# A guess of an expert computed outside the third attention, and three sums moved from GpSimd to VectorE, in a fused attention and mixture-of-experts kernel

## The chip, the core and the metric

The kernel runs on 1 core of one Trainium2 chip. The metric is the device time of one execution in microseconds (us). Before the change three runs took 357.07, 357.61 and 358.25 us; the median is 357.61.

## What is computed

The reference is grouped-query attention (8 batches, 16 heads of queries, 4 of keys and values, 384 positions, 64 per head), whose output goes, row by row, through a mixture of 4 × 4 experts with two gates. Cut to its core:

```python
scores = np.matmul(q, k.transpose(0, 1, 3, 2)) / np.sqrt(D)     # k, v repeated for 4 heads each
attn = np.exp(scores - scores.max(-1, keepdims=True))
x = np.matmul(attn / attn.sum(-1, keepdims=True), v)            # -> rows of 1024
g_idx = np.argmax(x @ w_group, axis=1)                          # a group, then an expert of it
e_idx = np.argmax(xg @ w_expert[g], axis=1)
ye = np.maximum(xg @ w1[g, e], 0.0) @ w2[g, e]
out[tok] = g_w * e_w * ye                                       # softmax weights of the two picks
```

## The kernel before

The work is staged by batch. The attention of a batch has 24 **units** (`NU`; 4 key heads times 6 blocks of 64 keys). A unit is a score step (`score`, L318: four 64x64 matmuls into a PSUM tile "s", then one exponential on ScalarE, L324, which writes `e`) and a product with v (`pv`, L337). `Attn.run` puts the score of unit u + 2 ahead of the product of unit u, so TensorE works while ScalarE takes exponentials; there are two "s" tiles, so the score of unit u + 2 can start only when the exponential of unit u has been read. "s" tiles are shared with the hidden layer and the output of the experts, "o" tiles with the outputs of attention. The name "x" gives the "o" tile that is not in use at that moment.

The sums of the softmax are taken from `e`: GpSimd adds the two units of a pair (`pair`, L345), VectorE reduces the pair (`reduce`, L354); units listed in `apart` are not added on GpSimd, and VectorE reduces both units of the pair itself (pair u holds units u - 1 and u). `join_keys` (L407) adds the parts, `sums` (L416) adds over partitions with TensorE and takes reciprocals, `normalise` (L455, L459) multiplies, `cast` (L464, or L466 on GpSimd) makes the bf16 copy `xb` that the experts read, a quarter of the 1024 columns at a time.

The experts' weights (2 MB each for w1 and w2) are loaded for one expert per batch, and that expert is *guessed* before the gate is known: the sum of v over the keys (`vsum`) goes through TensorE (`guess_mean`, L480), VectorE copies the result (`vm`, L482), TensorE multiplies it with the gate matrix (`guess_logits`, L487), VectorE picks the expert (`pick_guess`, L568 to L581) and GpSimd reads its number (`read_pick`) and issues the loads. Any pick of the real gate that the guess did not cover is computed in a loop at the end.

The order on every engine is written out by hand: the dictionaries `steps0`, `steps1` and `steps2` list what follows the product of a unit in the first three attentions (2: after unit 2; 4.5: after unit 4, ahead of its pair and reductions), `lags` says behind which unit a pair is reduced. The expert layers of batch b run behind the attention of batch b + 1, except the first hidden layer (`moe_h(0, ...)`), which stands in the second attention behind unit 17. `first_block` holds what lies between the second and the third attention: the first outputs of batch 0 (`ffn_y`, L650), the sums and the normalisation of batch 1, whose last two quarters GpSimd multiplies. `block(b)` is the same for the later batches. The gate's logits of batch 1 (`second_gate`, L474) stand in the third attention.

`sum_v` (L112 to L114) is the sum of v on GpSimd in three additions; `first_sum_v` (L121) the same on VectorE in one reduction, for batch 0 alone.

Of the kernel before, what the change touches and what calls it, by code (L numbers as in the profile page):

```python
# [18 lines left out]
def kernel(  # L19
# [97 lines left out]

    def first_sum_v():
        vsum[0] = gpool.tile([P, NA * D], BF16, name="vsum")
        with nc.allow_low_precision(reason="the guess of an expert alone reads this"):  # L120
            nc.vector.tensor_reduce(  # L121
                out=vsum[0].rearrange("p (a d) -> p a d", d=D),
                in_=vraw[0].rearrange("p a (c d) -> p a d c", d=D), axis=AX.X, op=ALU.add)

# [286 lines left out]

    def sums(b, g0, g1, which, tiles=False):
        sm = ps_tile(which)[:, :, :(g1 - g0) * 2 * NB]
        for r in range(2):
            if not tiles:
                nc.tensor.matmul(out=sm[:, r], lhsT=half32[:, r, :],  # L416
                                 rhs=red[b][:, g0:g1].rearrange("p g t j -> p (g t j)"),
                                 start=True, stop=True)
                continue
            rs = slice(r * H2, (r + 1) * H2)  # L420
            for t in range(2):
                nc.tensor.matmul(
                    out=sm[t * D:(t + 1) * D, r].rearrange("p (g t j) -> p g t j", t=2, j=NB)[:, :, t],
                    lhsT=half32[rs, r, t * D:(t + 1) * D], rhs=red[b][rs, g0:g1, t],
                    start=True, stop=True)
        if b not in inv:
            inv[b] = gpool.tile([P, KQ, NB], F32, name="inv", bufs=2)
        iv = inv[b][:, 2 * g0:2 * g1].rearrange("p (g r) j -> p r g j", r=2)
        sm = sm.rearrange("p r (g t j) -> p r g t j", t=2, j=NB)
        for t in range(2):  # L430
            ts = slice(t * D, (t + 1) * D)
            nc.vector.reciprocal(out=iv[ts], in_=sm[ts, :, :, t])  # L432

    Q = P // 4
# [35 lines left out]
    def gate_logits(b, pt):  # L470
        for m in range(KQ):
            x = xT[b][:, m, :].rearrange("p (j t x) -> p t j x", t=4, x=32)
            for t in range(4):
                nc.tensor.matmul(out=pt[32 * t:32 * t + 32, 0, :S // 4],  # L474
                                 lhsT=wg[:, head_pair(m), :], rhs=x[:, t],
                                 start=(m == 0), stop=(m == KQ - 1))

    def guess_mean(b, pt):
        pm = pt[:, 1, :2]
        nc.tensor.matmul(out=pm, lhsT=vsum[b], rhs=halfb, start=True, stop=True)  # L480
        vm = gpool.tile([P, 2], BF16, name="vm")
        nc.vector.tensor_copy(out=vm, in_=pm)  # L482
        return vm

# [147 lines left out]
    def ffn_h(x, w1, hT, f0, which):  # L632
        h = ps_tile(which)
        for jj in range(2):
            for m in range(KQ):
                nc.tensor.matmul(out=h[:, jj, :S],  # L636
                                 lhsT=w1[:, head_pair(m), (f0 + jj) * P:(f0 + jj + 1) * P],
                                 rhs=x[:, m, :], start=(m == 0), stop=(m == KQ - 1))
        if f0 + 2 < FQ:
# [41 lines left out]
    def before_attention(b):  # L681

        if b + 1 < B:
# [10 lines left out]
             for i in range(5)]  # L694
# [3 lines left out]
                      22: [17]}),  # L698
        1: Attn(1, apart=(9, 11), act_copies=(2, 3), later=(7, 13, 15, 17), homes=homes,
                lags={18: [13], 19: [15], 20: [17], 22: [19], 23: [21]}),  # L700
# [23 lines left out]
    def x_logits(b):  # L724
# [7 lines left out]
        0: [gate_matrix_2],  # L732
        2: [do(first_q1, "x"), first_sum_v],
        4: [do(first_k, NC, 2 * NC, "x")],
# [23 lines left out]
    def first_fetch():  # L758
# [18 lines left out]
            do(at[1].reduce, 3),  # L777
            do(at[1].reduce, 5),
            x_gate_logits,
            lambda: mean(1, state["pt"]),  # L780
            do(at[1].pair, 7),
            do(at[1].reduce, 7),
            do(moe_h, 0, 2, "s"),
            do(at[1].pair, 13),
            do(at[1].pair, 15),
            first_softmax,
            do(at[1].reduce, 9),
            do(moe_h, 0, 4, "s"),
# [10 lines left out]
    def first_block():  # L799
        load_v(3)  # L800
        moe_y(0, 0, "s")
        sum_v(2)
        load_k(3)
# [3 lines left out]
        y = ffn_y(w2s[0], hTs[0], 1, "s", (0,))  # L807
        sums(1, 0, Hkv, "o")
        ffn_y(w2s[0], hTs[0], 1, "s", (1,), y)
# [5 lines left out]
        ffn_y(w2s[0], hTs[0], 2, "o", (0,), y)  # L815
        at[2] = Attn(2, later=(1,), lags={5: [1], 6: [3], **{u: [u - 2] for u in range(7, NU, 2)}})
        at[2].score(0)
# [3 lines left out]
        normalise(1, 1, None, pool)  # L821
        normalise(1, 3, None, pool)

    def second_gate():
# [5 lines left out]
    steps2 = {  # L830
        1: [do(cast, 1, 2), do(at[2].pair, 1), do(x_mean, 2)],
        2: [do(x_logits, 2)],
        3: [do(cast, 1, 1)],
        4.5: [second_gate],
        6: [do(cast, 1, 3)],
        8: [do(read_pick, 2)],
    }
    at[2].run(steps2)
# [3 lines left out]
    def block(b):  # L842
# [24 lines left out]
        at[b].reduce(NU - 1)  # L867
        join_keys(b, 0, Hkv)
        if b == 2:
# [24 lines left out]
        if ahead:  # L894
            guess_logits(vm, guess_out(pt))
        elif not last:
            vm = guess_mean(b + 1, pt)
        ffn_y(w2s[f], hTs[f], 1, "s", (1,), y)
        y_out(f, 1, y)
        gate_logits(b, pt)  # L900
        if not (last or ahead):
            guess_logits(vm, guess_out(pt))
        if b <= EARLY:
            at[b + 1] = Attn(b + 1)
            at[b + 1].start()
        cast(b, 3)
        w = gate_softmax(b, gate_rows(pt, not last), not last)
# [166 lines left out]
```

## Time and profile before

| | us |
|---|---|
| median of three runs | 357.61 |
| the profiled execution | 356.7 |
| its span, first to last instruction | 354.9 |
| TensorE busy with matmuls | 345.9 (97%) |
| VectorE busy | 253.9 (72%) |
| ScalarE busy | 225.0 (63%) |
| GpSimd busy | 220.2 (62%) |

PE is TensorE's matmuls, PEld its weight loads, DVE VectorE, ACT ScalarE, POOL GpSimd, SP the engine that issues most loads and stores. Matmuls overlap, so the duration of one matmul is longer than the time from its start to the start of the next; what a matmul costs is read from start to start. "Busy" at 97% therefore leaves open whether the matmuls follow each other as fast as they could. A few matmul records are missing from the trace (one expert output block shows 7 or 22 where 8 or 23 were issued).

### The profile page before, as it was taken

The numbers are of one execution on the slowest core, as the hardware profiler recorded it, in microseconds if no ns is written. First come the engines' busy times: TensorE is split into PE (matmuls) and PEld (weight loads), VectorE is DVE, ScalarE is ACT, GpSimd is POOL, SyncE is SP. The second block draws the span as 40 slices with busy tenths as digits, with TensorE's granted clock in tenths as the row PEclk, the third lists the DMA queues.
The fourth block names the chain that finished last, engine by engine and source line by source line (L and its number), as shares of the span: only waits on it lengthen the run. The fifth ranks groups of instructions, "written<-read, shape, count | busy, mean of one in ns | idle before, by whom it ended". The sixth has DMA issues, their size and how long they took to land.

```text
span 354.9 us, 9208 instructions
## 1 busy us (share of the span) xinstructions
PE 345.9 (97%) x3801; PEld 182.5 (51%) x3816; DVE 253.9 (72%) x520; ACT 225.0 (63%) x296; POOL 220.2 (62%) x171
## 2 busy tenths in 40 slices
PE   8999999999999999999999999999999999999994
PEld 4455565445555455554555555545545545555642
DVE  5797769767697777976689667886769677796031
ACT  5899925299536795378954499355982669444311
POOL 7889985869935499308991299804995059900000
PEclk9999999999999999999999999999999999999998
DMA  8979999799989999999999999999995995099925
GB/s 199 215 135 188 220 207 160 134 275 222 193 174 176 258 209 182 206 163 203 229 221 207 193 220 211 218 192 193 228 211 95 197 263 130 2 175 219 258 48 137
DMA packets 69327, 67.15 MB, mean 189 GB/s; under 512 B 37113, under 2 KB 49401, under 8 KB 69281
## 3 DMA queue, kind: packets, MB, share of 16 engines
q0 software_dynamic: 26640, 41.03, 67.2%
q1 hardware_dynamic: 42272, 24.94, 30.4%
q8 instruction: 32, 0.52, 0.6%
q10 hardware_dynamic: 368, 0.54, 0.4%
q14 instruction: 15, 0.11, 0.1%
HBM read 86.07 MB, written 12.58 MB: 278 GB/s over the span
## 4 chain that ended last, share of the span: by engine, by line
PE 87%; ACT 4%; POOL 3%; DVE 2%; issue 1%; DMA 1%; ACTq 0%; SPq 0%; POOLq 0%; DVEq 0%
PE ps_o L337 30%; PE ps_s L636 22%; PE ps_s L650 13%; PE ps_s L318 8%; PE ps_o L650 6%; PE ps_o L474 3%; ACT e L324 2%; POOL w L345 2%; PE ps_o L636 1%; PE ps_s L951 1%; PE ps_o L951 1%; DMA w<-in_q_dram 1%; POOL xb L466 1%; ACT w L324 0%; DVE inv L432 0%
## 5 line engine op out<-in xcount | busy, mean ns | idle before, releaser
L345 POOL TENSOR_TENSOR e<-e 128x768 f32<-128x768 f32 x91 | 162.8, 1826 | 37.0 <-PE ps_s L318 30.8
L324 ACT ACTIVATE e<-ps_s 128x768 f32<-128x768 f32 x187 | 147.7, 813 | 15.0 <-PE ps_s L318 12.8
L337 PE MATMUL ps_o<-e,v_raw 64*64 64x384 f32 x1496 | 150.1, 482 | 0.0
L354 DVE TRANSPOSE_TENSOR_REDUCE red<-e 128x24 f32<-128x768 f32 x95 | 91.4, 972 | 36.7 <-POOL e L345 36.6
L636 PE MATMUL ps_s<-xb,w 128*128 128x384 bf16 x480 | 80.1, 326 | 0.1
L337 PEld LDWEIGHTS ps_o<-e,v_raw 64*64 64x64 f32 x1496 | 55.3, 133 | 35.7 <-issue 29.5
L636 PEld LDWEIGHTS <-w 128*128 128x128 bf16 x512 | 49.4, 98 | 36.4 <-issue 4.5
L318 PE MATMUL ps_s<-qT,kT 64*64 64x384 bf16 x768 | 65.0, 325 | 0.4
L650 PEld LDWEIGHTS <-hT 128*128 128x128 bf16 x336 | 31.5, 98 | 37.7 <-issue 1.5
L650 PE MATMUL ps_s<-w,hT 128*128 128x512 bf16 x217 | 49.5, 379 | 0.4
L640 ACT ACTIVATE hT<-ps_s 128x768 bf16<-128x768 f32 x23 | 18.6, 810 | 46.7 <-PE ps_s L636 43.3
L318 PEld LDWEIGHTS <-kT 64*64 64x64 bf16 x768 | 24.5, 105 | 35.6 <-issue 33.6
L669 ACT ACTIVATE ot<-ps_s,we 128x1024 f32<-128x1024 f32 x14 | 15.6, 1115 | 19.0 <-PE ps_s L650 17.2
L604 POOL COPY tok<-qT 1x1 bf16<-1x1 bf16 x6 | 1.1, 179 | 42.5 <-DMA qT<-q_raw 42.5
L379 DVE COPY xT<-ps_o 128x768 f32<-128x768 f32 x26 | 24.0, 924 | 2.7 <-ACT xb L464 1.5
L455 DVE STREAM_TRANSPOSE e<-inv 128x768 f32<-128x768 f32 x26 | 25.2, 971 | 0.2
L464 ACT CAST xb<-xT 128x768 bf16<-128x768 f32 x28 | 23.1, 830 | 3.4 <-DVE xT L459 3.2
L650 PE MATMUL ps_o<-w,hT 128*128 128x512 bf16 x105 | 24.0, 379 | 1.1 <-issue 1.1
L459 DVE TENSOR_TENSOR xT<-xT,e 128x768 f32<-128x768 f32 x24 | 23.1, 962 | 0.8
L495 DVE STREAM_TRANSPOSE gl<-ps_o 128x96 f32<-128x96 f32 x8 | 2.3, 283 | 18.7 <-PE ps_o L474 15.0
L643 ACT ACTIVATE hT<-ps_s 128x384 bf16<-128x384 f32 x14 | 6.1, 488 | 12.5 <-PE ps_o L480 7.2
L474 PEld LDWEIGHTS ps_o<-xT,wg 128*32 128x32 f32 x448 | 9.2, 110 | 3.3 <-issue 2.1
(140 smaller groups left out, 233.3 us busy)
## 6 DMA issues: line engine op xcount, KB each, us to landing
w<-in_moe_w_dram POOLq DMA_DIRECT2D x16, 2048.0 KB, 21.9
out_dram<-ot SPq DMA_DIRECT2D x42, 256.0 KB, 6.9
q_raw<-in_q_dram POOLq DMA_DIRECT2D x7, 768.0 KB, 11.0
v_raw<-in_v_dram SPq DMA_DIRECT2D x7, 384.0 KB, 5.7
k_raw<-in_k_dram POOLq DMA_DIRECT2D x7, 192.0 KB, 6.4
out_dram<-ot SPq DMA_DIRECT2D x10, 128.0 KB, 2.4
w<-in_q_dram POOLq DMA_DIRECT2D x3, 192.0 KB, 6.3
w<-in_k_dram SPq DMA_DIRECT2D x2, 192.0 KB, 3.7
```

What stands on the lines that cost most here:

```text
L318: nc.tensor.matmul(out=sT[r * H2:(r + 1) * H2, s, :S], lhsT=kT[b][s * D:(s + 1) * D, key_block(b, s, g // 2, c), ks], rhs=qT[b][s * D:(s + ...
L324: nc.scalar.activation(e.rearrange("p t (s x) -> p s t x", s=2), sT[:, :, :S].rearrange("p s (t x) -> p s t x", t=2), ACT.Exp, scale=scale)
L337: nc.tensor.matmul(out=oT[t * D:(t + 1) * D, r, :S], lhsT=vraw[b][r * H2:(r + 1) * H2, g // 2, c * D:(c + 1) * D], rhs=self.e[u][r * H2:(r ...
L345: nc.gpsimd.tensor_add(out=self.e[u - 1], in0=self.e[u - 1], in1=self.e[u])
L354: nc.vector.tensor_reduce(out=red3[b][:, g, parts[b][g]].rearrange("p t j -> p (t j)"), in_=self.e[w].rearrange("p t (j x) -> p (t j) x", ...
L379: nc.vector.tensor_copy(out=dst, in_=src)
L455: nc.vector.transpose(out=rb.rearrange("p k (j x) -> p k j x", x=32), in_=inv[b][:, ks].unsqueeze(3).to_broadcast([P, 2, NB, 32]))
L459: eng.tensor_mul(out=x, in0=x, in1=rb)
L464: nc.scalar.copy(out=xb[b][:, ks, :], in_=xT[b][:, ks, :])
L474: nc.tensor.matmul(out=pt[32 * t:32 * t + 32, 0, :S // 4], lhsT=wg[:, head_pair(m), :], rhs=x[:, t], start=(m == 0), stop=(m == KQ - 1))
L636: nc.tensor.matmul(out=h[:, jj, :S], lhsT=w1[:, head_pair(m), (f0 + jj) * P:(f0 + jj + 1) * P], rhs=x[:, m, :], start=(m == 0), stop=(m == ...
L650: nc.tensor.matmul(out=y[:, nh, :], lhsT=hT[:, f, c * P:(c + 1) * P], rhs=w2[:, f, nh * HALF:(nh + 1) * HALF], start=(f == 0), stop=(f == ...
```

## The change

- **`ffn_h`**: the first hidden block of a batch (`f0` = 0) is summed in two passes: six of eight row blocks of x for both halves of the tile, then the last two for both.
- **The sum of v for batch 2** is taken by VectorE (`reduce_v(2)`) in the second attention, behind unit 17 and ahead of `first_softmax`, in place of GpSimd's `sum_v(2)` in `first_block`. The reductions of units 8 and 9 move ahead of it too.
- **The guess for batch 2**: its product stands in the tile and beside the matmuls of `sums(1, ...)` in `first_block`; in the third attention only the logits are left, behind unit 1 in place of unit 2.
- **Pairs**: 23 of the second attention (units 22 and 23) and 1 of the third (units 0 and 1) are `apart`; the latter was put off by `later` before, and is now reduced behind unit 2.
- **Casts** of batch 1: three quarters, behind units 1, 3 and 6 before, now stand together behind the gate's logits at 4.5.
- **Batch 3's guess** in `block(2)`: product behind the gate's logits, logits behind the first two scores of the next attention.
- Keys of the third attention's first head are joined behind unit 10.

```diff
-    def first_sum_v():
-        vsum[0] = gpool.tile([P, NA * D], BF16, name="vsum")
+    def reduce_v(b):
+        vsum[b] = gpool.tile([P, NA * D], BF16, name="vsum")
...
-    def sums(b, g0, g1, which, tiles=False):
-        sm = ps_tile(which)[:, :, :(g1 - g0) * 2 * NB]
+    def sums(b, g0, g1, which, tiles=False, mean=None):
+        pt = ps_tile(which)
+        sm = pt[:, :, :(g1 - g0) * 2 * NB]
...
+        if mean is not None:
+            guess_product(mean, pt, MEAN)
...
+        return pt if mean is None else guess_copy(pt, MEAN)
...
+    MEAN = 2 * KQ * NB
+
+    def guess_product(b, pt, n):
+        nc.tensor.matmul(out=pt[:, 1, n:n + 2], lhsT=vsum[b], rhs=halfb, start=True, stop=True)
+
+    def guess_copy(pt, n):
+        vm = gpool.tile([P, 2], BF16, name="vm")
+        nc.vector.tensor_copy(out=vm, in_=pt[:, 1, n:n + 2])
+        return vm
...
-        for jj in range(2):
-            for m in range(KQ):
-                nc.tensor.matmul(out=h[:, jj, :S],
...
+        ends = [0, KQ] if f0 else [0, KQ - 2, KQ]
+        for m0, m1 in zip(ends, ends[1:]):
+            for jj in range(2):
+                for m in range(m0, m1):
+                    nc.tensor.matmul(out=h[:, jj, :S],
...
-        1: Attn(1, apart=(9, 11), act_copies=(2, 3), later=(7, 13, 15, 17), homes=homes,
+        1: Attn(1, apart=(9, 11, 23), act_copies=(2, 3), later=(7, 13, 15, 17), homes=homes,
...
+            do(at[1].reduce, 9),
             x_gate_logits,
             lambda: mean(1, state["pt"]),
             do(at[1].pair, 7),
             do(at[1].reduce, 7),
+            do(reduce_v, 2),
             do(moe_h, 0, 2, "s"),
             do(at[1].pair, 13),
             do(at[1].pair, 15),
             first_softmax,
-            do(at[1].reduce, 9),
...
-        sum_v(2)
...
-        sums(1, 0, Hkv, "o")
+        state["vm"] = sums(1, 0, Hkv, "o", mean=2)
...
-        at[2] = Attn(2, later=(1,), lags={5: [1], 6: [3], **{u: [u - 2] for u in range(7, NU, 2)}})
+        at[2] = Attn(2, apart=(1,), lags={6: [3], **{u: [u - 2] for u in range(7, NU, 2)}})
...
+    def second_logits():
+        state["pt"] = ps_tile("x")
+        x_logits(2)
...
-        1: [do(cast, 1, 2), do(at[2].pair, 1), do(x_mean, 2)],
-        2: [do(x_logits, 2)],
-        3: [do(cast, 1, 1)],
-        4.5: [second_gate],
-        6: [do(cast, 1, 3)],
+        1: [second_logits],
+        2: [do(at[2].reduce, 1)],
+        4.5: [second_gate, do(cast, 1, 2), do(cast, 1, 1), do(cast, 1, 3)],
         8: [do(read_pick, 2)],
+        10: [do(join_keys, 2, 0, 1)],
...
-        elif not last:
-            vm = guess_mean(b + 1, pt)
         ffn_y(w2s[f], hTs[f], 1, "s", (1,), y)
         y_out(f, 1, y)
         gate_logits(b, pt)
         if not (last or ahead):
-            guess_logits(vm, guess_out(pt))
+            vm = guess_mean(b + 1, pt)
         if b <= EARLY:
             at[b + 1] = Attn(b + 1)
             at[b + 1].start()
+        if not (last or ahead):
+            guess_logits(vm, guess_out(pt))
```

How this stands on the engines is shown at three places (the numbers behind a tile's name only tell tiles apart). First VectorE in the second attention, from the reductions of pairs 1, 3 and 5 to the softmax of batch 0, before:

```order
L354 TENSOR_REDUCE red_842<-w_87 128x24 x3
L482 CAST vm<-ps_o_846 128x2
L354 TENSOR_REDUCE red_842<-e 128x24
L495 STREAM_TRANSPOSE gl<-ps_o_846 128x96
L497 COPY gl<-ps_o_846 128x20
```

And the same place now:

```order
L354 TENSOR_REDUCE red_842<-w_87 128x24 x3
L354 TENSOR_REDUCE red_842<-e 128x24 x2
L489 CAST vm<-ps_o_848 128x2
L354 TENSOR_REDUCE red_842<-e 128x24
L121 TENSOR_REDUCE vsum<-v_raw 128x128
L506 STREAM_TRANSPOSE gl<-ps_o_848 128x96
```

Two reductions (units 8 and 9) have come ahead of the copy of batch 1's guess, and the sum of v of batch 2 ahead of the softmax. Next VectorE from the end of that softmax to the normalisation of batch 1 and the guess of batch 2, before:

```order
L599 CAST e_i<-ef 128x1
L354 TENSOR_REDUCE red_842<-e 128x24 x10
L407 TENSOR_REDUCE red<-red_842 128x24 x4
L432 RECIPROCAL inv<-ps_o_1116 64x2x4x12 x2
L455 STREAM_TRANSPOSE ps_o_1136<-inv 128x2x384
L459 TENSOR_TENSOR xT<-xT,ps_o_1136 128x768
L455 STREAM_TRANSPOSE ps_o_1139<-inv 128x2x384
L459 TENSOR_TENSOR xT<-xT,ps_o_1139 128x768
L455 STREAM_TRANSPOSE e<-inv 128x768 x2
L482 CAST vm<-ps_o_1213 128x2
L568 TENSOR_REDUCE km<-ps_o_1213 128x1
```

And now:

```order
L610 CAST e_i<-ef 128x1
L354 TENSOR_REDUCE red_842<-e 128x24 x9
L407 TENSOR_REDUCE red<-red_842 128x24 x4
L435 RECIPROCAL inv<-ps_o_1113 64x2x4x12 x2
L489 CAST vm<-ps_o_1113 128x2
L459 STREAM_TRANSPOSE ps_o_1136<-inv 128x2x384
L463 TENSOR_TENSOR xT<-xT,ps_o_1136 128x768
L459 STREAM_TRANSPOSE ps_o_1139<-inv 128x2x384
L463 TENSOR_TENSOR xT<-xT,ps_o_1139 128x768
L459 STREAM_TRANSPOSE e<-inv 128x768 x2
L579 TENSOR_REDUCE km<-ps_o_1211 128x1
```

Nine reductions stand where ten stood, and the copy of the guess (`vm`) has moved from behind the normalisation to ahead of it. Last ScalarE from the second exponential of the third attention on, before:

```order
L324 ACTIVATE e<-ps_s_1158 128x2x2x192
L669 ACTIVATE ot<-ps_o_1134,we 128x1024
L324 ACTIVATE e<-ps_s_1188 128x2x2x192
L324 ACTIVATE e<-ps_s_1200 128x2x2x192
L464 CAST xb<-xT 128x768
L324 ACTIVATE e<-ps_s_1217 128x2x2x192
L324 ACTIVATE e<-ps_s_1243 128x2x2x192
L464 CAST xb<-xT 128x768
L324 ACTIVATE e<-ps_s_1256 128x2x2x192
L324 ACTIVATE e<-ps_s_1301 128x2x2x192
L324 ACTIVATE e<-ps_s_1317 128x2x2x192
L464 CAST xb<-xT 128x768
```

And now:

```order
L324 ACTIVATE e<-ps_s_1158 128x2x2x192
L682 ACTIVATE ot<-ps_o_1134,we 128x1024
L324 ACTIVATE e<-ps_s_1188 128x2x2x192
L324 ACTIVATE e<-ps_s_1200 128x2x2x192
L324 ACTIVATE e<-ps_s_1227 128x2x2x192
L324 ACTIVATE e<-ps_s_1241 128x2x2x192
L324 ACTIVATE e<-ps_s_1253 128x2x2x192
L468 CAST xb<-xT 128x768 x3
L324 ACTIVATE e<-ps_s_1301 128x2x2x192
```

The three casts, which stood between exponentials at three places, now stand together behind the exponential of unit 6.

## Rows read from the trace of the kernel before

**Rows 1.** Windows: start:end, length, busy us of each engine, granted clock, DMA share, GB/s.

```profile
72.98:95.04 22.06, 21.79 (x349) 11.90 (x348) 14.71 (x25) 20.09 (x27) 21.16 (x12) 1.00 1.14 237
```

**Rows 2.** Timeline of PE, second attention: start, us, operation [idle before].

```profile
44.29 3.01 PE L636 MATMUL ps_s<-xb,w 128*128 128x384 bf16 x16
```

**Rows 3.** Chain of waits at the first hidden block: start, us, what.

```profile
44.66 0.82 POOL xb L466
...
45.52 1.78 PE ps_s L636 x10
...
48.87 2.62 PE ps_s L636 x16
```

**Rows 4.** Timeline of PE, third attention.

```profile
74.72 0.18 PE L480 MATMUL ps_o<-halfb,vsum 128*128 128x2 bf16 x1
74.95 0.36 PE L318 MATMUL ps_s<-qT,kT 64*64 64x384 bf16 x4
...
75.89 0.21 PE L487 MATMUL ps_o<-wg,vm 128*128 128x20 bf16 x2
76.03 0.36 PE L318 MATMUL ps_s<-qT,kT 64*64 64x384 bf16 x4
...
77.09 0.36 PE L318 MATMUL ps_s<-qT,kT 64*64 64x384 bf16 x4
...
78.16 1.53 PE L474 MATMUL ps_o<-xT,wg 128*32 128x96 f32 x64
79.61 0.36 PE L318 MATMUL ps_s<-qT,kT 64*64 64x384 bf16 x4
...
81.42 0.81 PE L337 MATMUL ps_o<-e,v_raw 64*64 64x384 f32 x8
...
82.22 0.81 PE L337 MATMUL ps_o<-e,v_raw 64*64 64x384 f32 x8
...
83.29 0.84 PE L337 MATMUL ps_o<-e,v_raw 64*64 64x384 f32 x8
```

**Rows 5.** Chain of waits through ScalarE in the third attention.

```profile
71.66 1.50 ACT e L324 x2
73.17 1.03 ACT ot L669
74.20 0.71 ACT e L324
...
81.64 0.72 ACT xb L464
```

**Rows 6.** Timeline of DVE, second attention to the sums of batch 1.

```profile
48.91 0.16 DVE L482 CAST vm<-ps_o 128x2 bf16<-128x2 f32 x1 [1.73 <-PE ps_o L480]
...
51.57 0.28 DVE L495 STREAM_TRANSPOSE gl<-ps_o 128x96 f32<-128x96 f32 x1 [1.62 <-PE ps_o L487]
...
55.97 7.85 DVE L354 TRANSPOSE_TENSOR_REDUCE red<-e 128x24 f32<-128x768 f32 x9
...
67.35 0.75 DVE L432 RECIPROCAL inv<-ps_o 64x96 f32<-64x96 f32 x1 [1.64 <-PE ps_o L416]
```

**Rows 7.** The line of VectorE's sum of v: duration ns min/median/max, starts.

```profile
L121 DVE TENSOR_REDUCE vsum<-v_raw x1: 1519/1519/1519, 11.3 to 11.3; 128x128 bf16<-128x768 f32 x1
```

**Rows 8.** Timeline of POOL, third attention.

```profile
73.88 3.59 POOL L459 TENSOR_TENSOR xT<-xT,e 128x768 f32<-128x768 f32 x2 [4.27 <-DVE e L455]
77.43 21.41 POOL L345 TENSOR_TENSOR e<-e 128x768 f32<-128x768 f32 x12
```

**Rows 9.** Timeline of PE and its weight loads, sums of batch 2.

```profile
98.62 1.79 PE L636 MATMUL ps_s<-xb,w 128*128 128x384 bf16 x10
...
100.42 0.52 PEld L416 LDWEIGHTS ps_o<-red,half 128*128 128x128 f32 x4 [0.39 <-DVE red L407]
```

**Rows 10.** DMA issues of 161.8 to 162.5 us: KB each, us to landing.

```profile
w<-in_moe_w_dram POOLq DMA_DIRECT2D x1, 2048.0 KB, 27.7
```

**Rows 11.** Timeline of PE, output of batch 3's experts.

```profile
190.85 1.46 PE L650 MATMUL ps_s<-w,hT 128*128 128x512 bf16 x5
```

More of the change, by code (lines that the diff above doesn't have):

```diff
@@ L116, in sum_v @@
         vsum[b] = t
-    def first_sum_v():
-        vsum[0] = gpool.tile([P, NA * D], BF16, name="vsum")
+    def reduce_v(b):
+        vsum[b] = gpool.tile([P, NA * D], BF16, name="vsum")
         with nc.allow_low_precision(reason="the guess of an expert alone reads this"):
             nc.vector.tensor_reduce(
-                out=vsum[0].rearrange("p (a d) -> p a d", d=D),
-                in_=vraw[0].rearrange("p a (c d) -> p a d c", d=D), axis=AX.X, op=ALU.add)
+                out=vsum[b].rearrange("p (a d) -> p a d", d=D),
+                in_=vraw[b].rearrange("p a (c d) -> p a d c", d=D), axis=AX.X, op=ALU.add)
     def new_qT(b):
@@ L476, in gate_logits @@
                                  start=(m == 0), stop=(m == KQ - 1))
-    def guess_mean(b, pt):
[L479 to L483, printed above, removed]
+    MEAN = 2 * KQ * NB
[5 more added lines that the diff above has]
+        return vm
+    def guess_mean(b, pt):
+        guess_product(b, pt, 0)
+        return guess_copy(pt, 0)
     def guess_logits(vm, out_):
@@ L633, in ffn_h @@
         h = ps_tile(which)
-        for jj in range(2):
-            for m in range(KQ):
-                nc.tensor.matmul(out=h[:, jj, :S],
-                                 lhsT=w1[:, head_pair(m), (f0 + jj) * P:(f0 + jj + 1) * P],
-                                 rhs=x[:, m, :], start=(m == 0), stop=(m == KQ - 1))
+        ends = [0, KQ] if f0 else [0, KQ - 2, KQ]
[3 more added lines that the diff above has]
+                    nc.tensor.matmul(out=h[:, jj, :S],
+                                     lhsT=w1[:, head_pair(m), (f0 + jj) * P:(f0 + jj + 1) * P],
+                                     rhs=x[:, m, :], start=(m == 0), stop=(m == KQ - 1))
         if f0 + 2 < FQ:
@@ L732 @@
         0: [gate_matrix_2],
-        2: [do(first_q1, "x"), first_sum_v],
+        2: [do(first_q1, "x"), do(reduce_v, 0)],
         4: [do(first_k, NC, 2 * NC, "x")],
@@ L867, in block @@
         at[b].reduce(NU - 1)
-        join_keys(b, 0, Hkv)
+        join_keys(b, int(b == 2), Hkv)
         if b == 2:
```

## The prediction, made before the changed kernel was run

> **What bounds the kernel now.** I read the table of engines first: TensorE has a matmul under way for nearly the whole span. [...] So there is no large wait to remove; a gain must come from places where TensorE's matmuls start later than the matmul ahead of them allows. I found those by reading start times in TensorE's timeline and asking the chain of waits who released them. Once the pipeline runs, a unit of attention (four score matmuls, eight with v) takes 0.80 us from start to start (81.42 to 82.22, [rows 4]), and a 384-column matmul of the experts takes 2.62/16 = 0.164 us (sixteen in a row from 48.87, [rows 3]). I call every start that is later than these figures a loss. Since the matmuls of the later batches follow each other at these rates with nothing waiting in between, a microsecond won before them should stay won.
>
> **Part by part.**
>
> *The first expert layer in two passes over the halves of its sum (ffn_h).* In the second attention the first hidden block starts at 44.29. Six matmuls later it needs the fourth quarter of xb, which GpSimd's cast delivers at 44.66 + 0.82 = 45.48; the next matmul starts at 45.52 [rows 2, 3]. Without the wait it would have started at 44.29 + 6 × 0.164 = 45.27, so the loss is 0.25 us. In the new order twelve matmuls need only the first three quarters and last until 44.29 + 12 × 0.164 = 46.26, after the cast. **-0.25**, all on the path. In the other seven batches the casts are long done; there the edit only changes the order of the same matmuls. I cost that at nothing. Its bounds: 0, since both halves of the tile were written one after the other before without a visible gap, and 0.01 us, the last digit of a row, for each of two more changes of half in eight batches, 0.16.
>
> *The sum of v on VectorE.* The one reduction of this shape took 1519 ns [rows 7]; it goes ahead of the first softmax, together with the two reductions of units 8 and 9, 7.85/9 = 0.87 each [rows 6]. VectorE sat idle there twice, 1.73 and 1.62 us, for TensorE's guess product and guess logits [rows 6]. TensorE comes 0.25 earlier, so 1.48 and 1.37 are left for 1.74 and 1.52: the softmax starts at most 0.1 us after TensorE's logits. TensorE doesn't wait for the softmax; cost nothing. On GpSimd three additions go, off the path.
>
> *Units 22 and 23 reduced apart.* VectorE does two reductions for one (+0.87), no longer behind GpSimd's last pair; two others have left the same queue (units 8 and 9), so nine stand behind the softmax where ten stood. VectorE waited 1.64 us for TensorE's sums of this batch [rows 6], and by the time TensorE reaches them VectorE is done again. Cost nothing; if that cover went, each microsecond beyond about 1.0 (1.64 less the sums' own 0.6) would be paid in full. GpSimd issues the next two weight loads one pair earlier, 21.41/12 = 1.78 us [rows 8].
>
> *The third attention.* Before, from the guess product at 74.72 to the score at 79.61 TensorE spends 4.89 us [rows 4]. Needed are three units and the gate's logits: 3 × 0.80 + 1.45 (78.16 to 79.61) = 3.87. The loss of 1.02 is the guess product and the score behind it (74.72 to 74.95), the guess logits, a score at 77.09 that waits until ScalarE has done a cast ahead of its exponential, and the gate's logits, which at 78.16 have waited for the choice of an expert in the same PSUM tile. A second cast costs 83.29 - 82.22 - 0.80 = 0.27 further on [rows 4, 5]. Together 1.29. After the change the product stands beside the sums of the batch ahead, where no tile shape changes (0.03 at most). Left are the guess logits, 0.14 (75.89 to 76.03); what ScalarE still holds up; and the three casts in one block:
> - ScalarE runs two exponentials (1.50), the output scaling (1.03) and the next exponential (0.71) without a gap, and the score at 74.95 starts 0.04 after that [rows 5, 4]. So ScalarE, too, sets this score. Its chain starts at VectorE's normalisation, which comes 0.25 earlier with TensorE, less up to 0.16 for the copy of the guess (the copy at 48.91 took that, [rows 6]) now in front of it. I take 0.15 earlier, 74.80; TensorE would be ready at 74.72 - 0.22 + 0.14 = 74.64. Wait 0.16.
> - Let the gate's logits start at G. The exponential ahead of the casts ends about G + 0.3; three casts at 0.72 (81.64, [rows 5]) last to G + 2.46, and the exponential behind them to G + 3.25. The score that needs it could start at G + 1.45 + 2 × 0.80 = G + 3.05. Wait 0.2. Two casts and the last quarters of the gate also need GpSimd's products, which end at 73.88 + 3.59 = 77.47 before [rows 8], somewhat earlier now, against G at about 77.2 and a need at G + 1.0: no wait.
>
> Loss after: 0.14 + 0.16 + 0.2 = 0.5. **-0.79**; bounds -0.3 (the casts uncovered as before: 0.5 more) and -1.15.
>
> *The sums of batch 2.* TensorE's weight loading stood 0.39 us until VectorE joined the keys at 100.42; by the matmuls ahead the place was free at 98.62 + 10 × 0.164 = 100.26 [rows 9]. The joining hangs on GpSimd's last pair, twelve of which ran back to back [rows 8]; there are eleven now, so it is 1.8 us earlier while TensorE is about 1.0 earlier. I take **-0.2**; bounds 0 and -0.39.
>
> *The guess of batch 3 moved behind the gate's logits, its logits behind two scores.* The same matmuls in another place, with as many changes of tile shape; by the costs of 74.72 and 75.89 [rows 4] within 0.1 either way. I take 0.
>
> **Sum:** -0.25 - 0.79 - 0.2 = -1.24. The profiled execution took 356.7 us with a span of 354.9; it becomes 355.5 with 353.7. It was 0.9 under the median of the runs, 357.61 (357.07 to 358.25); from the median, 357.61 - 1.24 = 356.4.
>
> [...]
>
> **Rivals.**
> 1. *ScalarE gives the casts' time back.* The block of three casts is not hidden by the gate's logits, or GpSimd's products come as late as before; then only the first part and a bound of the third attention are left: -0.25 - 0.3 = -0.55, 357.1. For it: ScalarE is busy 20.09 of 22.06 us there [rows 1]. Against: one exponential behind another takes 0.75 and a unit of TensorE 0.80, so ScalarE catches up.
> 2. *The weights set the time further on.* The second weights of batch 3 were on their way 27.7 us from 161.65, to 189.35 [rows 10]; TensorE used them at 190.85 [rows 11]. The margin of 1.5 us holds 1.24 if the transfer doesn't move at all. If it lands later by 1 us, because the loads that now start 1.8 us earlier meet others, 0.75 is given back: 357.1; by 1.5 us, all of it: 357.6. Against: the whole row of loads starts earlier.
> [...]
> 4. *The change doesn't do what it says:* two of the three guess matmuls stay in the third attention, and ScalarE still sets the scores around them. Then the third attention wins nothing: -0.25 - 0.2, 357.2.
>
> **How the numbers follow.** The forecast 0.58, rival 1 0.17, rival 2 0.09, rival 3 0.06, rival 4 0.10. A measurement of this kernel can tell about 0.3% (1.07 us) from no change. The forecast lies at 0.35%, not far over that: of its 0.58 I give 0.44 to faster by over 0.3% and 0.14 to no change; a late transfer that loses nothing adds little, so faster is 0.47. Slower are rival 3 and 0.02 of rival 2: 0.08. The same is left with 0.45. The forecast's own range is -0.7 to -1.75 us (the ends of the third attention and of the sums of batch 2), 355.9 to 356.9. To hold 8 in 10 it reaches over rivals 1 and 4: 355.7 to 357.4.
>
> **What would show it.** In the first hidden block no matmul starts late, sixteen of them in 2.6 us. In the third attention no guess product; from the score behind the guess logits to the one behind the gate's logits about 3.9 us; three casts in a row on ScalarE at the gate's logits, and the score two units behind them late by some 0.2 at most. The sums of batch 2 without idle time ahead of their weights. VectorE's sum of v at about 1.5 us, and still a wait of VectorE for TensorE at the sums of batch 1. Wrong it would be if TensorE waits there for VectorE, if a matmul of the later batches waits for weights, or if the periods of the later batches change.

## The result, and the profile after

The changed kernel took 361.46 us (median of five runs, 359.35 to 362.03; a sixth took 362.97), the kernel before 357.56 beside it: a ratio of 1.0108, 95% interval 1.0072 to 1.0144. It is slower; forecast was 356.4, and the range ended at 357.4. The profiled execution took 359.35 with a span of 357.6, against 354.9 before.

Where the 2.7 us came from is read in the windows between the same places of the program: the first hidden block of batch 0, the first of batch 1, of batch 2 and of batch 3. Columns as in [rows 1]. First the kernel before, then the changed one:

```profile
44.29:95.04 50.75, 50.17 (x605) 27.00 (x603) 37.49 (x74) 32.62 (x44) 41.48 (x30) 1.00 1.05 200
95.04:137.96 42.92, 42.70 (x474) 22.22 (x472) 32.66 (x69) 27.66 (x37) 28.67 (x22) 1.00 1.12 199
137.96:180.42 42.46, 42.25 (x478) 21.98 (x476) 32.33 (x64) 29.03 (x38) 26.50 (x20) 1.00 1.08 200
```

```profile
45.30:95.19 49.89, 49.73 (x607) 27.46 (x603) 42.03 (x79) 32.60 (x44) 37.11 (x27) 1.00 1.06 203
95.19:137.82 42.63, 42.63 (x475) 22.26 (x472) 32.48 (x69) 27.74 (x37) 26.95 (x21) 1.00 1.05 196
137.82:183.09 45.27, 42.64 (x480) 21.90 (x476) 31.52 (x64) 28.91 (x38) 27.12 (x20) 1.00 1.07 191
```

The first two stretches, which the change is about, became shorter by 0.86 and 0.29 us, 1.15 together. The third, in which the change edits nothing that TensorE waited for, became longer by 2.81. The rest is the start: the first hidden block began at 45.30 in place of 44.29. Over all traces of this study it began at 44.3 to 44.6 where the warm-up and the order were those of before, and at 44.4 to 45.3 in versions of the changed kernel with that warm-up; that the change has a part in the late start is not shown. 1.01 - 0.86 - 0.29 + 2.81 = 2.67 of 2.7.

The places that the prediction spoke of, in the changed kernel. PE's timeline, first hidden block, against [rows 2, 3]: sixteen matmuls and no late one, the gate's logits 2.71 us after the block's start.

```profile
45.30 2.77 PE L649 MATMUL ps_s<-xb,w 128*128 128x384 bf16 x16
48.01 1.53 PE L478 MATMUL ps_o<-w,wg 128*32 128x96 f32 x64
```

PE's timeline, third attention, against [rows 4]: no guess product; the score behind the guess logits at 75.88, 0.46 later than a unit's 0.80 behind the one at 74.62; the one two units behind the gate's logits 0.17 late (79.89 to 81.66, less 1.60).

```profile
74.62 0.34 PE L318 MATMUL ps_s<-qT,kT 64*64 64x384 bf16 x4
...
75.54 0.21 PE L498 MATMUL ps_o<-wg,vm 128*128 128x20 bf16 x2
75.88 0.36 PE L318 MATMUL ps_s<-qT,kT 64*64 64x384 bf16 x4
...
78.43 1.53 PE L478 MATMUL ps_o<-xT,wg 128*32 128x96 f32 x64
79.89 0.36 PE L318 MATMUL ps_s<-qT,kT 64*64 64x384 bf16 x4
...
81.66 0.36 PE L318 MATMUL ps_s<-qT,kT 64*64 64x384 bf16 x4
```

ACT's timeline there, against [rows 5]: the three casts stand in one row, with exponentials at 0.74 to 0.75 on both sides.

```profile
75.01 3.70 ACT L324 ACTIVATE e<-ps_s 128x768 f32<-128x768 f32 x5
78.61 2.29 ACT L468 CAST xb<-xT 128x768 bf16<-128x768 f32 x3
80.80 3.75 ACT L324 ACTIVATE e<-ps_s 128x768 f32<-128x768 f32 x5
```

DVE's timeline, against [rows 6, 7]: the sum of v took 1.47, and VectorE still waited 1.40 for TensorE's sums of batch 1.

```profile
50.85 1.47 DVE L121 TENSOR_REDUCE vsum<-v_raw 128x128 bf16<-128x768 f32 x1
...
68.14 1.52 DVE L435 RECIPROCAL inv<-ps_o 64x96 f32<-64x96 f32 x2 [1.40 <-PE ps_o L485]
```

PE's weight loads at the sums of batch 2, against [rows 9]: no idle time ahead of them.

```profile
100.24 0.58 PEld L417 LDWEIGHTS ps_o<-red,half 128*128 128x128 f32 x4
```

The loss is one wait. The chain of waits of the changed kernel, 136 to 152 us (start, us, what):

```profile
139.57 7.11 DMA qT<-q_raw
...
147.24 0.89 POOL q_raw L101
...
148.15 1.02 POOL vs L112
...
149.24 1.21 POOL vs L113
...
150.52 0.46 POOL vsum L114
...
151.03 0.18 PE ps_o L485
```

TensorE's guess product of batch 4 needs the sum of v, which GpSimd does after it has started the load of batch 5's queries, and this load waits until the transposes of batch 4's queries have let go of the buffer. In the kernel before the chain at this place is TensorE alone, and GpSimd's timeline shows the same instructions done 1.8 us ahead of the product at 148.37:

```profile
141.31 0.74 POOL L96 DMA_DIRECT2D k_raw<-in_k_dram  x1
143.54 0.89 POOL L101 DMA_DIRECT2D q_raw<-in_q_dram  x1 [1.50 <-DMA qT<-q_raw]
144.45 1.01 POOL L112 TENSOR_TENSOR vs<-v_raw 128x384 f32<-128x384 f32 x1
145.54 0.47 POOL L113 TENSOR_TENSOR vs<-vs 128x128 f32<-128x128 f32 x1
146.09 0.47 POOL L114 TENSOR_TENSOR vsum<-vs 128x128 bf16<-128x128 f32 x1
```

So GpSimd was 3.7 us later with this load (147.24 against 143.54), and another 0.7 later at the end of the sum (150.97 against 146.56): the second addition took 1.20 us in place of 0.47, which the section on the prediction takes up. The transfers say why the load was late. The view of DMA issues (operation, count, us from issue to landing) for the transposes of batch 3's queries and of batch 4's, first the kernel before, then the changed one:

```profile
qT<-q_raw SPq DMA_TRANSPOSE x1, 5.5
...
qT<-q_raw SPq DMA_TRANSPOSE x1, 5.6
```

```profile
qT<-q_raw SPq DMA_TRANSPOSE x1, 7.2
...
qT<-q_raw SPq DMA_TRANSPOSE x1, 7.1
```

Each took 1.5 to 1.7 us longer. They were also issued later, the first by 0.63 us (98.92 against 98.29), which the late start can account for. The first delay passes on whole, because GpSimd starts the weights of batch 2 only when these transposes have landed (issued at 106.73, before 104.45), and everything behind the weights on that queue moves with them.

What stood in the way the first time is in the packets. The transposes' last data packet ended at 103.32 before and at 104.06 after, and each of them ends with 32 packets of 4 bytes, its completions. In the kernel before all are written by 103.33. In the changed kernel 28 are by 103.93, two at 104.25 and two at 105.02: behind an instruction fetch of 8,192 bytes (103.94 to 104.25) and one of 16,384 (104.05 to 105.02). So the last completion came 1.0 us behind the last data. GpSimd went on 1.1 us after it, in the kernel before 0.5; these 0.6 I can't place. The queue table of the second one's microsecond, changed kernel (packets, MB, share of the 16 engines); in the same microsecond behind the transposes' last packet the kernel before has no row q8 (there the fetch came at 104.80):

```profile
q1 hardware_dynamic: 104, 0.15, 73.3%
q8 instruction: 1, 0.02, 6.0%
```

The second time no fetch is near. There the load of batch 5's keys, which GpSimd issues when its pairs are done, had its first packets (144.65) ahead of the completions (145.56 to 146.35; the last data packet had ended at 144.59). In the kernel before the transposes ended at 142.50, 1.2 us behind that load's issue, the completions came at once, and the load's first packet followed at 142.74.

### The profile page after: what moved, and what is told of

Read it like the earlier page. It is cut to its first block, busy times and chain, and to the rows that moved or that the text cites. A ratio compares the mean times of both kernels' runs of the same rounds, so it can differ in the third digit from the quotient of the medians.

```text
span 357.6 us, 9223 instructions
## 1 busy us (share of the span) xinstructions
PE 347.7 (97%) x3816; PEld 183.3 (51%) x3816; DVE 259.3 (73%) x524; ACT 225.1 (63%) x296; POOL 214.9 (60%) x166
## 4 chain that ended last, share of the span: by engine, by line
PE 90%; POOL 2%; ACT 2%; DMA 2%; DVE 1%; issue 1%; ACTq 0%; POOLq 0%; DVEq 0%
PE ps_o L337 32%; PE ps_s L649 19%; PE ps_s L663 14%; PE ps_s L318 9%; PE ps_o L663 6%; PE ps_o L478 3%; DMA qT<-q_raw 2%; PE ps_o L649 1%; PE ps_s L967 1%; POOL e L345 1%; ACT e L324 1%; PE ps_o L967 1%; PE ps_o L277 1%; PE ps_o L259 1%; DVE eback L231 1%
## 5 line engine op out<-in xcount | busy, mean ns | idle before, releaser
L345 POOL TENSOR_TENSOR e<-e 128x768 f32<-128x768 f32 x89 | 159.1, 1819 | 31.9 <-PE ps_s L318 30.7
L354 DVE TRANSPOSE_TENSOR_REDUCE red<-e 128x24 f32<-128x768 f32 x97 | 93.4, 972 | 38.5 <-POOL e L345 38.2
L663 PE MATMUL ps_o<-w,hT 128*128 128x512 bf16 x112 | 25.5, 380 | 0.0
L463 DVE TENSOR_TENSOR xT<-xT,e 128x768 f32<-128x768 f32 x24 | 23.7, 987 | 0.8
L506 DVE STREAM_TRANSPOSE gl<-ps_o 128x96 f32<-128x96 f32 x8 | 2.3, 283 | 15.5 <-PE ps_o L478 15.1
```

The lines of the kernel that those rows point to most:

```text
L345: nc.gpsimd.tensor_add(out=self.e[u - 1], in0=self.e[u - 1], in1=self.e[u])
L354: nc.vector.tensor_reduce(out=red3[b][:, g, parts[b][g]].rearrange("p t j -> p (t j)"), in_=self.e[w].rearrange("p t (j x) -> p (t j) x", ...
L463: eng.tensor_mul(out=x, in0=x, in1=rb)
L663: nc.tensor.matmul(out=y[:, nh, :], lhsT=hT[:, f, c * P:(c + 1) * P], rhs=w2[:, f, nh * HALF:(nh + 1) * HALF], start=(f == 0), stop=(f == ...
```

## Experiments

The theory (T, F in the expectations): TensorE's lead took up most of the 1.8 us to spare at that product; an instruction fetch among the completions of one transfer delays the weights, the delayed transposes run into the next load, and the sum of v comes too late. Its rivals: chance, the exchange between VectorE and GpSimd, and TensorE's lead alone.

**The changed kernel again.**

> The changed kernel once more, for a second trace of it. Theory T (TensorE waits at the guess product of batch 4 for GpSimd's sum of v, which is queued behind the load of batch 5's queries, and that load waits for the transposes of batch 4's queries): the wait at that product is there again, 2 us or more, and the load of the queries is again held for over 3 us; time 359 to 362. Rival N (the wait of the first trace came from that execution's late start alone, everything on the DMA queues being 1.2 us late from the first weights on): with an ordinary start the product waits under 0.5 us, and the executions that took 361 to 362 lose their time at another place, which this trace would show.

360.36 us (359.10 to 362.63), ratio 1.0085 (1.0056 to 1.0114). The traced execution waits at the same product, and both transposes landed after 7.2 and 7.3 us. This execution began late too (45.00), so by itself it leaves the late start as a cause; the version below that began at 44.50 and lost 1.8 us at the same product does not. Chance falls. The waits of PE:

```profile
PE ps_o L485 <- POOL vsum L114: 2.7, 1, 2.7
```

**The sum of v ahead of the loads**, in the changed kernel and in the kernel before:

```
 else:
+    if b == EARLY:
+        sum_v(b + 1)
     if b + 2 < B:
         load_k(b + 2)
         load_q(b + 2)
-    if not last:
+    if not (last or b == EARLY):
         sum_v(b + 1)
```

> The changed kernel with GpSimd's sum of v for batch 4 ahead of the two loads for batch 5 in its queue; nothing else is altered. Theory T: the sum ends at about 144.5 us, some 4 us before TensorE needs it, the wait of 2.6 us is gone, and with it whatever follows from it: 356 to 357, faster than the kernel before by 0.5 to 1.3 us. Rival W (the transfers as a whole are late, and the second weights of batch 3 would stop TensorE next): the wait moves to the second expert layer of batch 3 at about 190 us, 1 us or more, and the time stays above 358.

357.52 us (355.71 to 361.55, twelve runs), ratio 0.9988 (0.9970 to 1.0007): the 3 to 4 us are gone, the gain isn't there. Theory T holds for the first part. GpSimd's timeline shows the sum done at 142.87, and a second thing: with the load of the keys issued 1.2 us later, 1.5 us ahead of the transposes' end, these landed in 5.5 us.

```profile
142.42 0.45 POOL L114 TENSOR_TENSOR vsum<-vs 128x128 bf16<-128x128 f32 x1
142.99 0.74 POOL L96 DMA_DIRECT2D k_raw<-in_k_dram  x1
145.56 0.89 POOL L101 DMA_DIRECT2D q_raw<-in_q_dram  x1 [1.84 <-DMA qT<-q_raw]
```

And rival W has a part. PE's timeline has the second layer of batch 3 late by 0.7 us:

```profile
190.33 0.17 PE L485 MATMUL ps_o<-halfb,vsum 128*128 128x2 bf16 x1
191.05 2.12 PE L663 MATMUL ps_s<-w,hT 128*128 128x512 bf16 x8 [0.56 <-ACT hT L656]
```

The row names ScalarE, but the first matmuls don't read its last tile, and the row of their weight load (PEld) names the weights:

```profile
191.05 1.84 PEld L663 LDWEIGHTS <-hT 128*128 128x128 bf16 x10 [0.78 <-DMA w<-in_moe_w_dram]
```

The last packet of the weights ended at 190.13, and the lead of 0.5 us on the kernel before at 180 us is gone at 222.

> The kernel before with GpSimd's sum of v for batch 4 ahead of the two loads for batch 5. Theory T: the kernel before has 1.8 us to spare at that product (the sum ends at 146.56, the product starts at 148.37), so nothing is won: 357.0 to 358.0, the same. Its trace up to that place is a second sample of when the transposes of the kernel before land: around 103.9 and 143.5 us. If the kernel before too loses time there in some executions, this one is faster by up to 0.5 us.

357.01 us, ratio 0.9991 (0.9978 to 1.0004): the same, as expected. Transposes landed in 5.5 and 5.6 us.

**The sum of v for batch 2 back on GpSimd.**

```
     moe_y(0, 0, "s")
+    sum_v(2)
     load_k(3)
...
-    do(reduce_v, 2),
```

> The changed kernel with the sum of v for batch 2 back on GpSimd, ahead of the loads of k and q for batch 3; the rest of the change stays. Rival X (the exchange between VectorE and GpSimd makes the transfers late, because these loads are then issued 1.8 us earlier): the load of batch 5's queries is held no longer than before, about 1.5 us, the wait at the guess product of batch 4 is gone or under 0.5 us, time 356 to 357. Theory T with the lead of TensorE as its cause: the wait stays at 1.5 us or more, time 359 to 362.

358.09 us (356.44 to 360.55), ratio 1.0015 (0.9991 to 1.0038). The load of batch 5's queries was still held 4.5 us and TensorE lost 1.8 at its product, so rival X falls; the time expected for T was too high. TensorE's lead was nearly gone here (44.50 to 95.35 is 50.85 us, as long as before; the product of batch 2 waited 0.8 for GpSimd), and the transposes still took 6.5 and 7.4 us. That also speaks against the lead as what delays the transfers.

**The fetch moved, other things equal.** In the kernel before, twenty instructions more in TensorE's warm-up:

```
-    for i, n in enumerate((4, 4, 4, 4, 4, 4, 4, 1, 1)):
+    for i, n in enumerate((4, 4, 4, 4, 4, 4, 4) + (1,) * 12):
```

> The kernel before with ten more small matmuls (128 columns, 20 instructions with their weight loads) in the warm-up at the very start, and nothing else. Theory F (the transfers of the changed kernel fall behind at batch 3's queries because TensorE's 16,384-byte instruction fetch comes some 0.7 us earlier in its stream and gets in among the last completions of the transposes; GpSimd then starts the weights of batch 2 1.5 us later, its next load of k runs into the next transposes, and TensorE waits for the sum of v): the same fetch now comes among or before those completions, the weights of batch 2 are issued at 106 us in place of 104.5, the load of batch 5's queries is held over 3 us, TensorE waits 0.5 to 1.5 us at the guess product of batch 4: 358 to 359.5. Rival L (the lead of TensorE alone does it): the transfers stay as they are, weights at 104.5 to 105, time 357.0 to 358.3 with at most the few tenths of the longer warm-up.

360.66 us, ratio 1.0089 (1.0066 to 1.0113): ten matmuls that compute nothing cost 3.0 us, where the change cost 3.9. In the traces it is 3.3 us, of which 1.05 stand ahead of the first hidden block (45.34 against 44.29) and 1.5 are the wait at the product. The fetch starts at 104.35, where the last data packet of the transposes ends; both transposes landed in 7.2 us. The queue table of that microsecond:

```profile
q1 hardware_dynamic: 133, 0.20, 75.8%
q8 instruction: 1, 0.02, 6.0%
```

The weights of batch 2 were issued at 107.02, the sum of v ended at 151.32, and the product that could have started at 149.9 (10.4 us behind the first hidden block of batch 2, as before) started at 151.37. The product's own row names VectorE there, as it does in two other runs; the row of its weight load names the sum:

```profile
151.37 0.10 PEld L480 LDWEIGHTS <-vsum 128*128 128x128 bf16 x1 [1.71 <-POOL vsum L114]
```

TensorE had no lead in this kernel (it began 0.8 to 1.05 us late), so rival L falls as the only cause.

In the changed kernel, fewer:

```
-    for i, n in enumerate((4, 4, 4, 4, 4, 4, 4, 1, 1)):
-        nc.tensor.matmul(out=warm[:, i % 2, :n * P], lhsT=onesb, ...
+    onesf = onesb.bitcast(F32)
+    for i in range(2):
+        nc.tensor.matmul(out=warm[:P // 2, i, :4 * P], lhsT=onesf, ...
```

> The changed kernel with the nine warm-up matmuls at the very start replaced by two longer ones (float32, 512 columns, about the same time), 14 instructions fewer ahead of everything else on TensorE. Theory F: the 16,384-byte fetch comes about 1 us later, behind the last completions of the transposes of batch 3's queries; the weights of batch 2 are issued at about 105, the load of batch 5's queries is held at most 2 us, the wait at the guess product of batch 4 is under 0.8 us: 356 to 357.5. Rival L: the fetch moves and the wait stays at 2 us or more, time 359 to 361.

361.27 us, ratio 1.0103 (1.0078 to 1.0128). It tells nothing apart: the two float32 matmuls are recorded as four with four weight loads, so only ten instructions went, and the fetch stood at 104.66, again where the transposes' last packet ended; they landed in 7.2 and 7.5 us.

Then 96 instructions more, which bring the fetch ahead of the transposes, in the changed kernel, the kernel before, and the changed kernel with the sum first:

```
+    step = HALF // 2 if w2 is w2s[0] else HALF
     for nh in nhs:
+        for n0 in range(0, HALF, step):
             for f in range(FQ):
-                nc.tensor.matmul(out=y[:, nh, :], ...
+                nc.tensor.matmul(out=y[:, nh, n0:n0 + step], ...
```

> The kernel before with the same 96 instructions. Theory F: the fetch comes ahead of the transposes and harms nothing, 357.3 to 357.9, where twenty instructions more in the warm-up cost 3 us. Rival (any longer instruction stream on TensorE costs time, by itself or by waits for instructions): 359 or more.

357.10 us, ratio 0.9999 (0.9988 to 1.0009). Not more instructions cost time, but where their fetch falls: it is at 96.37 here, and the transposes landed in 5.5 and 5.5 us.

> The changed kernel with the 48 matmuls of the second expert layer of batch 0 split into two of 256 columns each: the same columns, 96 instructions more on TensorE between 62 and 75 us, which puts the 16,384-byte fetch of about 104 us some 8 us earlier, ahead of the transposes of batch 3's queries. Theory F: nothing stands among the last completions of those transposes, the weights of batch 2 are issued 1.1 to 1.2 us after their last packet (about 104.8 to 105.2), the load of batch 5's queries is held at most 2 us, the wait at the guess product of batch 4 is under 0.8 us; 356.2 to 357.4. Rival L (the lead of TensorE upsets the transfers): wait of 2 us or more, 359 to 361, wherever the fetch comes.

359.33 us, ratio 1.0066 (1.0046 to 1.0086): better by 1 to 2 us than the changed kernel, and not what theory F expected. The 16,384-byte fetch is at 96.62, but the 8,192-byte one still stands at 103.48 among the completions (the last two at 103.79, 0.2 behind the last data), and the transposes took 6.4 us, 0.9 over the usual: 0.2 by that fetch, and again 0.6 until GpSimd went on. The weights left at 105.55, 0.4 late by the expectation; GpSimd, early with TensorE, issued the keys at 140.79, 2.5 us ahead of the transposes' end, and those took 7.4. TensorE lost 2.0 at the product. So the lead seems to have a part in the second delay here; the two runs without a lead that had this delay show that it isn't needed.

Over the thirteen traces in which GpSimd waits for the transposes (all but one, which comes last but one) the second delay goes by one number, the time from the issue of the keys' load to the last data packet of the transposes: with 1.5 us or less (or the load behind) they landed in 5.5 to 5.6 us, seven times; with 2.2 to 2.9 in 7.1 to 7.5, six times.

> The same 96 instructions in the changed kernel with GpSimd's sum of v for batch 4 first. Theory F: neither the wait for that sum nor the one for the second weights of batch 3; the whole lead of 1.15 us that TensorE has at 138 us reaches the end: 356.2 to 356.8, faster than both kernels. Rival W: the weights of batch 3 are late all the same, 357 to 358.

356.68 us (355.57 to 361.14, twelve runs), ratio 0.9978 (0.9963 to 0.9993): faster than both kernels, than the kernel before by 0.2%. The wait at the product is gone. The chain of waits has what is left, the second weights of batch 3, 0.6 us late:

```profile
162.88 27.80 DMA w<-in_moe_w_dram
...
190.72 2.33 PE ps_s L665 x10
```

And the same for the second layer of batch 1:

```
-    step = HALF // 2 if w2 is w2s[0] else HALF
+    step = HALF // 2 if w2 is w2s[0] or w2 is w2s.get(1) else HALF
```

> The changed kernel with GpSimd's sum of v for batch 4 first and the second expert layers of batches 0 and 1 in matmuls of 256 columns (192 instructions more in all). In the version with 96 more, the next 16,384-byte fetch stood at 159.34 us, again at the end of transposes (those of batch 5's queries, 159.35), the weights of batch 3 were issued at 162.0 and TensorE waited 0.6 us for the second of them at 190.7. Theory F: the fetch comes ahead of these transposes, the weights are issued at about 160.5 to 161.2, the wait at 190 us is at most 0.2 us, and the median falls by 0.3 to 0.6, to 356.1 to 356.4. Rival W (the weights are late whatever the fetch does, since they are bound by what their queue carries): the wait stays at 0.5 us or more, 356.6 to 357.

356.59 us (356.15 to 357.52), ratio 0.9980 (0.9969 to 0.9991). The fetch is at 156.02 and no longer at the transposes' end, which landed in 5.7 in place of 7.1 us, but the weights left only 0.46 earlier, 161.55, landed at 190.62, and TensorE lost 0.6 us again; the narrower matmuls of batch 1 cost 0.5. The weights were 28.55 us on their way in place of 27.80, which took the earlier start back. Rival W holds in that these weights bound this version with TensorE 0.5 us ahead of the kernel before (its product at 190.38 against 190.83); why they took longer is not shown.

**No wait for the transposes ahead of batch 2's weights**, in the version with the sum first:

```
-    after_transposes(b + 1)
+    if b != 2:
+        after_transposes(b + 1)
```

> The changed kernel with GpSimd's sum of v for batch 4 first, and without GpSimd's wait for the transposes of batch 3's queries ahead of the loads of the weights of batch 2 (the small copy that makes it wait is left out; the data don't need it). If late transfers are all that holds this version back: the weights of batch 2 start at about 99, land at 131 to 132 in place of 134.3, those of batch 3 at 187 to 189 in place of 190.1, no wait at 191 us, time 355.8 to 356.6 with less spread: faster than the kernel before by about 1.2. Rival: the transposes, now beside the weights, take so much longer that k and q of batch 4 land no earlier; time 357 to 358 as without this edit.

372.25 us, ratio 1.0406 (1.0383 to 1.0429): wrong by both theories. The weights left at 97.88, and the transposes of batch 3's queries, issued at 98.98, landed 28.9 us later. The waits of PE:

```profile
PE ps_s L318 <- DMA qT<-q_raw: 13.5, 1, 13.5
```

From 118 to 130 us, in that wait and just behind it, the granted clock was 0.50; over the whole span it was 0.975, against 0.996 in the version with the wait for the transposes. Of the 15.5 us by which the span is longer (371.1 against 355.6) 13.5 are TensorE's wait; what the lower clock cost of the rest was not taken apart. The wait of GpSimd's, which passes every delay of the transposes on, is therefore needed in this order of loads.

**The split of the first hidden block alone** (the change's edit of ffn_h), in the kernel before:

> The kernel before with only the first hidden block of each expert in two passes over the halves of its sum. The prediction's first term: no late matmul in the first hidden block of batch 0, and TensorE 0.25 us earlier from there to the next place where it waits; 357.1 to 357.5 if that lasts to the end. If a lead of TensorE by itself upsets the transfers, the load of batch 5's queries is held longer than 1.5 us and the time is 357.6 or more.

357.40 us, ratio 0.9996 (0.9983 to 1.0008). Between the first hidden blocks, the window of its trace against 50.75 before:

```profile
44.55:95.05 50.50, 50.21 (x607) 26.99 (x603) 37.80 (x74) 32.61 (x44) 41.45 (x30) 1.00 1.06 200
```

Of these 0.25 us only 0.09 were left at the first hidden block of batch 2 (138.13, that is 93.58 us behind the first, against 93.67). The other 0.16 went at the gate's logits of batch 2, which wait for VectorE; one of its multiplications ahead of them took 1.52 us there and 1.03 in the kernel before. The weight loads of these logits, the kernel before and this run:

```profile
113.17 1.31 PEld L474 LDWEIGHTS ps_o<-xT,wg 128*32 128x32 f32 x64 [0.42 <-DVE vm L482]
```

```profile
113.34 1.31 PEld L474 LDWEIGHTS ps_o<-xT,wg 128*32 128x32 f32 x64 [0.59 <-DVE vm L482]
```

The load of batch 5's queries was held 1.70 us here, 0.2 more than in the kernel before, and the transposes landed in 5.5 and 5.6 as there: a lead of this size did next to nothing to the transfers.

## Why the prediction was wrong

*The steps that were right.* The split was to give 0.25 us: it gave 0.25 by itself. The sums of batch 2 were to give 0.2, with the moved guess of batch 3 at 0: the stretch became shorter by 0.29. VectorE kept its cover; the sum of v took 1.47 where 1.52 was taken, and the guess product beside the sums of batch 1 took 0.03 (67.92 to 67.95), the bound that was set for it. Rival 3, with 0.06 of the chances, was that VectorE becomes the bound there because its moved work waits for GpSimd. No row of the changed kernel shows such a wait: the moved reductions cost their own time beside GpSimd's pairs, 0.90 each (two from 48.12 took 1.79).

*VectorE and GpSimd did slow each other, at another place:* where VectorE's multiplications of the normalisation (L463, two inputs) meet GpSimd's additions. Alone the multiplication took 0.96 us, 309 times in all traces, and the second addition of a sum of v 0.45 to 0.51; where the two meet the addition took 1.05 to 1.27, in 19 of 19, and the multiplication up to 2.04. VectorE in the changed kernel, and in the version with 96 instructions more:

```profile
149.17 0.96 DVE L463 TENSOR_TENSOR xT<-xT,e 128x768 f32<-128x768 f32 x1
```

```profile
146.89 2.04 DVE L463 TENSOR_TENSOR xT<-xT,e 128x768 f32<-128x768 f32 x1
```

The first ends at 150.13, and the addition that had started at 149.24 ended at 150.44. So the late sum of v ran into these multiplications, and 0.7 of the 2.65 us that TensorE waited came from there.

*A term that was mis-sized.* The third attention was to give 0.79 and gave 0.86 - 0.25 = 0.61. ScalarE held the score behind the guess logits for 0.32 us (0.46 less the logits' 0.14), not 0.16. The casts cost 0.17 against 0.2. (The forecast's own range was written as -0.7 to -1.75; the bounds of its terms add up to -0.55 and -1.79. Neither reaches the result.) In all 1.15 against 1.24 had been won when the third stretch began.

*The step that failed* stands in the first part: since the later matmuls follow each other with nothing waiting in between, "a microsecond won before them should stay won". That TensorE waits for nothing there doesn't say by how little. Rival 2 asked this of one arrival, the weights of batch 3, and took the transfers as fixed or earlier ("the whole row of loads starts earlier"). There was a nearer margin: the sum of v for batch 4, 146.56 against 148.37, at the end of a chain that doesn't move with TensorE (transposes, a load, GpSimd). Counted from the start of the first hidden block, the change spends 1.15 of these 1.81 us, and the sum ended 3.4 later: 2.7 by the transfers, which were taken as fixed, and 0.7 by the longer addition. By the clock, with the start 1.01 later, these are 0.14, 3.7 and 0.7. The run of the split shows another such place with nothing to spare, the gate's logits of batch 2. With transfers on time the kernel should have kept its gain as far as the weights; nearest to that is the version with the sum first and the fetch moved, 356.7.

*Slower for another reason than rival 3.* Of the 0.08 for slower 0.06 were on VectorE, which stayed idle where it was to be, and 0.02 on the weights of batch 3. Rival 2 let loads that the edit moves delay these weights, at worst to no gain; no rival let an edit on TensorE delay the transposes.

*What stays open.* Which of the edits moves the fetch: with the split alone it stayed behind the completions (104.91), and with the sum back on GpSimd it still stood among the last data (103.32). That leaves the other edits, which were not run alone. And why most executions of the changed kernel took up to 3.6 us more than the two that were traced (359.35 and 359.55): the granted clock is lower in most of them (0.987 to 0.995; 0.996 and 0.999 in the traced ones), but not in all, and none has a trace. The one trace in which the clock fell clearly is that with a wait of 13.5 us.

## What to carry to other kernels

Where an engine is busy throughout, list for every place at which it takes something over how early that arrives, and follow the smallest of these margins back to transfers: a gain is kept only up to the least margin among arrivals that don't move with it, here 1.8 us at a sum that no wait pointed to. When one transfer's completion starts the next, look at what else is queued on the DMA engines just as it ends, the instruction stream too; a few instructions more or less far away can cost more than the edit brings (here twenty cost 3.0 us, where the change had won 1.15). And test a surprising loss with an edit that computes nothing: ten idle matmuls told more here than undoing the parts.

## What the runs showed of the hardware

Instruction fetches are DMA packets among the others: q8 carried 32 of 16,384 bytes, and since adding TensorE instructions moved them (104.80 to 96.37 with 96 more) they are TensorE's. For TensorE itself no cost shows: the kernel before with 96 instructions more took 357.10 us, ratio 0.9999. For another transfer one shows: with one fetch of 0.97 us between the last data and the last completions the transposes landed 1.7 us later, 1.0 by the packets and 0.6 until GpSimd went on. In all five traces in which the first transposes landed in 7.2 us the fetch began within 0.01 us of the end of the last data packet, and three fetches that began 0.06 to 0.26 us ahead of such an end held up no completion. So the fetch may itself have stood behind the transposes' data, and need not have been asked for just then; no run shows when it was.

A load's first packets between a transfer's data and its completions went with a landing 1.5 to 1.9 us later, in six traces of six. Why the completions came only behind these packets, and behind the fetch, no run shows.

Loads of 2,048-byte packets beside transposes of 256-byte ones went with a far later landing of these: the transposes of batch 3's queries, 5.5 to 7.2 us from issue to landing in the other traces, took 28.9.
